# A written list of visits, relu evictions over two banks, and x loads as words of the list

## The chip, the core and the metric

The kernel runs on one core of one Trainium2 chip. The metric is the device time of one launch in microseconds. Before the change three runs took 314.47, 314.52 and 314.9 us (median 314.52).

## The reference

Two stages, of which the second takes the first's output as its tokens:

```python
# x: (4, 12544, 128), inducing: (32, 128), w1, w2: (128, 1024), w_out: (1024, 128)
def mab(q, kv):
    s = scale * (q @ kv.transpose(0, 2, 1))
    s = s - s.max(-1, keepdims=True)
    a = np.exp(s)
    a /= a.sum(-1, keepdims=True) + 1e-09
    return a @ kv
h = mab(I, x)                     # 32 inducing points look at all of x, per batch
attn = mab(x, h)                  # each token looks at the 32 rows of h
g = np.maximum(attn @ w1, attn @ w2)
out = g @ w_out
```

With max(a, b) = a + relu(b - a) the second stage is attn @ (w1 @ w_out) + relu(attn @ (w2 - w1)) @ w_out. Since attn is e2 / sum(e2) times h, with e2 the exponentials of 32 scores per token, the kernel multiplies h into the weights first: hwd = h @ (w2 - w1), 32 x 1024 per batch, and m1 = h @ (w1 @ w_out), 32 x 128. The division by sum(e2) is left to the end.

## The kernel before

A batch has 98 chunks of 128 tokens. Tokens are worked on in 28 blocks of up to 16 chunks. In a block each of the four row tiles of TensorE (32 of its 128 rows, called a quarter q) has its own 4 chunks, or fewer in the blocks at the ends of batches: the 32 scores per token of quarter q lie on partitions 32q to 32q + 31 of the tile `e2`.

The work of one block, by the letters of the list:

- `s` (`stage`, L698 on): scores of the block on TensorE in four column tiles, then one exponential on ACT into `e2`.
- `p` (`phase`): a visit to the row tiles. Up to four units, one per quarter, each a product of 32 rows of `hwd` with `e2`, 512 columns, into a PSUM bank of its own. Matmuls of different quarters run side by side, those of one quarter one after the other. Each unit's bank is then evicted with a relu into `relus` in SBUF: on ACT (L1110) or, where the bit of the word's second number is set, on DVE (L1107). 784 units in all. With fewer than four units, a visit also takes along the linear part `m1` of one open group, 4 short matmuls on that group's row tile (L1205 records both).
- a number n: n products of the final matmul (`final_one`, L989), relu chunk (128 x 128) times a 128 x 128 piece of w_out, over all 128 rows. The products of one quarter of one block are a group: 8 per chunk, 3136 in all, 108 groups, each in a PSUM bank. When the group's linear part is in as well, `evict_group` multiplies by the reciprocal sums into one of 6 buffers (`osbs`) on DVE (L1024) or ACT (L1031), and SP stores it.
- `g` (`turn_e2`): SP turns `e2` by a DMA transpose, GpSimd adds up the 32 exponentials per token and takes the reciprocal (L776, L780). Blocks without it have their sums from TensorE and DVE instead (`dens`, L819, L829).
- `c`, `r`, `t`, `a`, `e`, `h`, `w`, `m`: the first stage of the next batch, its scores (L399) and exponentials (L413), their transposes, the sum over x (L458), then h, hwd and m1. `x` turns a piece of x into `xT`, a DMA transpose on SP. `H`, `V`, `W` are batch 0's last part of hwd, the turn of w1 and its product with w_out.

TensorE thus changes between three ways of working: over all rows, in row tiles, in column tiles. The order of TensorE's work, and with it that of all engines, is the string `ORDER`. Which units a visit takes and which PSUM banks everything uses is not in the string: `Clock` keeps expected times of the engines and banks while the program is generated, `pick` takes the units needed first, and each takes the bank that is expected to come free first. Where the clock expects a wait, `keep_busy`, `dummies` and `fill` put empty matmuls (L945, L619).

The loads of x come from GpSimd as DMAs that cast to 16 bits, 7 per batch, into a ring of 12 buffers; buffer (7b + i) % 12 holds part i of batch b. Batch 1's are issued in the head of the program. Those of batch b + 1 for b = 1 and 2 stand at the end of `pool_accum` (word `a1.5`, `a2.5`), all seven together, behind a small copy of the sum just made (`pace`), so that GpSimd does not run ahead of them.

The eviction of one unit, with the bank in `src` and the home of the block's quarter in `dst`:

```python
dst = blk.relu[q][:, 0 : NJB * w4 * 128].rearrange("p (j t) -> p j t", j=NJB)
dst = dst[:, u * jpb : (u + n) * jpb, 128 * t0 : 128 * (t0 + w)]
src = psall[:, bi, :].rearrange("p (j t) -> p j t", j=jpb)
nc.scalar.activation(out=dst, in_=src, func=AF.Relu)
```

`phase` has a third number that would hold a unit back and evict it with the same quarter's next one; no word of `ORDER` uses it.

Of the kernel before, what the change touches and what calls it, by code (L numbers as in the profile page):

```python
# [9 lines left out]
F16 = mybir.dt.float16  # L10
# [6 lines left out]
INF = 1e9  # L17
# [90 lines left out]
class Quarter:  # L108


    def __init__(self, b, c0, w):
        self.b, self.c0, self.w = b, c0, w
        self.subs = {1: [1], 2: [2], 3: [2, 1], 4: [4]}[w]


class Block:


    def __init__(self, quarters, full=()):
        self.quarters = quarters  # L120
        self.width = max(qu.w for qu in quarters if qu)
        self.b = [qu.b for qu in quarters if qu][0]
        self.staged = None
        self.first = None
        self.divided = 0.0
        self.rp = None
        self.units = []
        self.done = {}
        self.relu = {}
        self.last_group = {}  # L130
        self.groups = []
        for q, qu in enumerate(quarters):
            jobs = []
            t0 = 0
            for w in qu.subs if qu else []:
                for u in range(2 * w):
                    jobs.append((q, t0, w, u))
                t0 += w
            self.units.append(jobs)
            if qu:  # L140
                self.groups.append(Group(self, [(q, t) for t in range(qu.w)], q in full))


class Group:
    def __init__(self, blk, chunks, full):
        self.blk, self.chunks, self.full = blk, chunks, full
        self.q = chunks[0][0]
        self.bank = self.ps = None
        self.started = self.linear = False
        self.order, self.parts = [], []  # L150
        for q, t0, w, u in blk.units[self.q]:
            jpb = 4 // w
            self.parts.append((t0, u))
            self.order += [(jpb * u + jj, t0 + t) for jj in range(jpb) for t in range(w)]
# [3 lines left out]
def kernel(  # L158
# [37 lines left out]
    relus = [big.tile([128, 2, 4096], F16, name=f"relus{q}", tag=f"relus{q}") for q in range(4)]  # L196
    relu1 = [big.tile([128, 1024], F16, name=f"relu1_{q}", tag=f"relu1_{q}") for q in range(2)]
    osbs = big.tile([128, NOUT, 4, C], F32, name="osbs", tag="osbs")

# [23 lines left out]
    def load_x(b, i, after=None):  # L223
        k0, n = parts[b][i]
        if after is not None:

            nc.gpsimd.tensor_copy(out=pace, in_=after)
        nc.gpsimd.dma_start(out=xn_at[b, i][:, 0:n, :], in_=xr[b, :, k0 : k0 + n, :])  # L228
        if b:
            issued = ck.on_pool(ck.pe, 0.55)  # L230
            if i == 0 and b > 1:
                ck.loading = issued - 0.55
            st[b]["ld", i] = ck.loading + 6.3 + 2.72 * i if b > 1 else 25.7 + 2.5 * i
# [4 lines left out]
    def transpose_x_dma(b, j):  # L238
# [3 lines left out]
        landed = ck.on_sp(st[b]["ld", i], "x7" if n == 7 else "x14")  # L242
        for k in range(k0, k0 + n):
            st[b]["T", k] = landed

    identity16 = consts.tile([128, 128], F16, name="identity16")
    head16 = relus[3][:, 0, :]
# [10 lines left out]
    wf = relus[0][:, 0, :].bitcast(F32)  # L258
    w1f, w2f = wf[:, 0:J], wf[:, J : 2 * J]
    w1s = relus[1][:, 0, :]  # L260
# [8 lines left out]
    pace = consts.tile([128, 1], F32, name="pace")  # L269

    with tc.manual_schedule(engines={ET.PE, ET.DVE, ET.Activation, ET.Pool, ET.SP}):

        xf = relus[2][:, 0, 0 : 256 * P1].bitcast(F32)
# [119 lines left out]
        def pool_scores(b, u):  # L393
            if u == 0:
                st[b]["es"] = smp.tile([128, NU], F32, name=f"es_{b}", tag="esu")
            bi, ps = bank([128, 512])
            ck.wait(ck.bank[bi], "p1")
# [10 lines left out]
            ck.feed(8)  # L408
            end = ck.run(0.226, "col")
# [3 lines left out]
            nc.scalar.activation(  # L413
                out=eu, in_=ps, func=AF.Exp, scale=scale, accum_out=st[b]["es"][:, u : u + 1]
            )
            ck.bank[bi] = ck.on_act(end, 0.575)
            st[b]["eu", u] = eu, ck.bank[bi]

        def pool_rest(b):

            bi, ps = bank([128, 512])
            ck.wait(ck.bank[bi], "p1")
# [8 lines left out]
            end = ck.run(0.029 * REST)  # L431
            et = etp.tile([128, P1, M], F16, name=f"et_{b}", tag="et")
            nc.scalar.activation(out=et[:, 0:REST, :], in_=ps[:, 0 : REST * M], func=AF.Exp, scale=scale)
            ck.bank[bi] = ck.on_act(end, 0.2)
            st[b]["et"] = et, ck.bank[bi]

        def pool_turn(b, u):
            eT = etp.tile([128, 8, 128], F16, name=f"eT_{b}_{u}", tag="eT", bufs=NEU)
            nc.sync.dma_start_transpose(eT, st[b]["pair", u // 2].rearrange("p v (j t) -> p (v j) t", j=4))
            st[b]["eT", u] = eT, ck.on_sp(st[b]["eu", u][1], "eT")  # L440

        def pool_accum(b, u):

            bi, ps = bank([128, 512])
            ck.wait(ck.bank[bi], "p1")
# [4 lines left out]
            if last:  # L450
                nc.vector.reduce_sum(out=acc[:, C : C + 1], in_=st[b]["es"], axis=AX.X)
                ck.on_dve(st[b]["eu", u][1], 0.1)
            eT = st[b]["eT", u][0]
            st[b]["sum", u] = True
# [12 lines left out]
            if last:  # L467
                et = st[b]["et"][0]
# [17 lines left out]
            ck.feed(64)  # L486
            end = ck.run(0.58 if last else 0.49, "col")
# [5 lines left out]
            ck.bank[bi] = ck.on_dve(end, 0.22)  # L493
            if last:
                st[b]["esrr"] = ck.bank[bi]
# [4 lines left out]
        def small_rep(b):  # L500

            bi, ps = bank([128, 512])
            ck.wait(ck.bank[bi], "p1")
            nc.tensor.matmul(out=ps[:, 0 : C + 1], lhsT=repd, rhs=st[b]["hacc"], start=True, stop=True)  # L504
            end = ck.run(0.28)
# [5 lines left out]
            ck.bank[bi] = st[b]["haccr"] = ck.on_dve(end, 0.45)  # L511

        def small_h(b):
            hT4 = smp.tile([C, 4, M], F16, name=f"hT4_{b}", tag="hT4")
# [808 lines left out]
```

## Time and profile before

| | |
|---|---|
| timed runs | 314.47, 314.52, 314.9 us |
| the profiled execution: span, first to last instruction | 312.9 us |
| granted TensorE clock, mean | 0.998 |
| TensorE busy | 306.0 us |
| DVE busy | 273.1 us |
| ACT busy | 280.7 us |
| GpSimd busy | 122.6 us |
| HBM read and written | 27.28 and 25.69 MB |
| issues of x loads in the head, first and last | 19.6 and 26.2 us (batch 1) |

The profile's own execution has no separate time; its span stands for it, and the timed runs lie 1.6 us above the span. In a row of a group, the numbers behind the bar are the busy time in us, the mean duration of one instruction in ns, and the idle time of the engine just before such instructions with what ended it. In a row of the timeline stand the start, the time until the last of the row's instructions ends, the engine, and how many instructions of that kind followed each other. TensorE's durations overlap: the distance from one row's start to the next is what a piece of work takes.

### The profile page before, as it was taken

The numbers are of one execution on the slowest core, as the hardware profiler recorded it, in microseconds if no ns is written. First come the engines' busy times: TensorE is split into PE (matmuls) and PEld (weight loads), VectorE is DVE, ScalarE is ACT, GpSimd is POOL, SyncE is SP. The second block draws the span as 40 slices with busy tenths as digits, with TensorE's granted clock in tenths as the row PEclk, the third lists the DMA queues.
The fourth block names the chain that finished last, engine by engine and source line by source line (L and its number), as shares of the span: only waits on it lengthen the run. The fifth ranks groups of instructions, "written<-read, shape, count | busy, mean of one in ns | idle before, by whom it ended". The sixth has DMA issues, their size and how long they took to land.

```text
span 312.9 us, 12567 instructions
## 1 busy us (share of the span) xinstructions
PE 306.0 (98%) x5316; PEld 239.4 (77%) x5316; DVE 273.1 (87%) x485; ACT 280.7 (90%) x581; POOL 122.6 (39%) x183
## 2 busy tenths in 40 slices
PE   6999999999999999999999999999999999999996
PEld 2875777777877777778877887778778877788885
DVE  2458999999889999988999998999999899989894
ACT  3668999999989989999999999989999899998875
POOL 7374007910530006677500565139205743288000
PEclk9999999999999999999999999999999999999999
DMA  7999999999399999989699999993422522342223
GB/s 206 208 255 203 218 214 192 167 231 232 107 204 244 256 212 202 212 199 218 136 241 256 185 241 200 194 229 114 131 86 103 153 102 87 118 130 103 103 88 136
DMA packets 80793, 55.69 MB, mean 178 GB/s; under 512 B 62272, under 2 KB 65632, under 8 KB 80736
## 3 DMA queue, kind: packets, MB, share of 16 engines
q1 hardware_dynamic: 74768, 41.19, 56.5%
q0 software_dynamic: 5968, 13.70, 22.6%
q8 instruction: 41, 0.67, 0.9%
q14 instruction: 16, 0.13, 0.1%
HBM read 27.28 MB, written 25.69 MB: 169 GB/s over the span
## 4 chain that ended last, share of the span: by engine, by line
PE 94%; DMA 3%; DVE 1%; issue 1%; POOL 0%; ACT 0%; POOLq 0%
PE psall L989 61%; PE psall L1205 23%; DMA xn<-in_x_dram 3%; PE psall L712 2%; PE psall L458 1%; PE psall L399 1%; PE psall L309 1%; PE psall L371 1%; PE psall L325 1%; DVE relus L1107 1%; PE psall L571 1%; PE psall L504 0%; PE psall L362 0%; DVE hwd L575 0%; PE psall L819 0%
## 5 line engine op out<-in xcount | busy, mean ns | idle before, releaser
L1110 ACT ACTIVATE relus<-psall 128x512 f16<-128x512 f32 x468 | 239.2, 620 | 15.4 <-PE psall L1205 14.4
L1107 DVE TENSOR_SCALAR relus<-psall 128x512 f16<-128x512 f32 x308 | 195.5, 683 | 16.6 <-PE psall L1205 15.7
L989 PE MATMUL psall<-woutp,relus 128*128 128x128 f16 x3104 | 203.7, 220 | 0.0
L989 PEld LDWEIGHTS <-relus 128*128 128x128 f16 x3104 | 174.9, 98 | 33.1 <-issue 27.3
L1205 PE MATMUL psall<-e,hwd 32*128 32x512 f16 (+2 forms) x840 | 81.1, 362 | 0.0
L776 POOL TENSOR_TENSOR half<-ed 128x256 f32<-128x256 f16 (+2 forms) x22 | 13.4, 611 | 145.5 <-DMA ed<-e 145.5
L780 POOL TENSOR_TENSOR rd<-den,minus 128x16 f32<-128x16 f32 (+2 forms) x22 | 57.8, 2628 | 1.7
L1024 DVE TENSOR_TENSOR osbs<-psall,rd 128x512 f32<-128x512 f32 (+1 forms) x80 | 50.9, 637 | 4.3 <-PE psall L1205 1.3
L1205 PEld LDWEIGHTS <-hwd 32*128 32x128 f16 x880 | 27.9, 91 | 11.7 <-issue 2.3
L1205 PE MATMUL psall<-m,e 32*128 32x128 f16 x372 | 36.6, 216 | 0.0
L1205 PEld LDWEIGHTS <-e 32*128 32x128 f16 x372 | 22.2, 92 | 9.6 <-issue 2.0
L776 POOL TENSOR_TENSOR half<-half 128x32 f32<-128x32 f32 (+4 forms) x66 | 21.4, 324 | 5.2
L228 POOL DMA_DIRECT2D xn<-in_x_dram x32 | 17.8, 569 | 5.7 <-DMA xn<-in_x_dram 4.3
L1024 DVE TENSOR_TENSOR osbs<-psall,rp 128x512 f32<-128x512 f32 (+3 forms) x24 | 15.6, 649 | 0.5 <-PE psall L1205 0.4
L313 DVE COPY xT<-psall 128x512 f16<-128x512 f16 (+3 forms) x12 | 5.7, 485 | 8.6 <-PE psall L309 8.4
L413 ACT ACTIVATE eu<-psall 128x512 f16<-128x512 f32 x18 | 10.8, 612 | 0.3 <-PE psall L399 0.2
L725 ACT ACTIVATE e<-psall 128x512 f16<-128x512 f32 (+2 forms) x21 | 10.9, 574 | 0.1
L316 ACT COPY xT<-psall 128x768 f16<-128x768 f16 (+3 forms) x10 | 5.8, 576 | 4.6 <-PE psall L309 4.5
L309 PE MATMUL psall<-identity,xn 128*128 128x128 f16 x98 | 7.5, 219 | 1.5 <-DMA xn<-in_x_dram 1.0
L712 PE MATMUL psall<-xT,hT 128*32 128x512 f16 (+3 forms) x110 | 8.4, 362 | 0.0
L309 PEld LDWEIGHTS <-xn 128*128 128x128 f16 x98 | 5.5, 97 | 3.1 <-DMA xn<-in_x_dram 1.4
L399 PE MATMUL psall<-xT,inducingT 128*32 128x512 f16 x72 | 6.4, 381 | 0.0
(114 smaller groups left out, 129.8 us busy)
## 6 DMA issues: line engine op xcount, KB each, us to landing
out_dram<-osbs SPq DMA_DIRECT2D x90, 256.0 KB, 2.9
xn<-in_x_dram POOLq DMA_DIRECT2D x24, 448.0 KB, 9.9
out_dram<-osbs SPq DMA_DIRECT2D x10, 128.0 KB, 4.3
relus<-in_moe_w_dram POOLq DMA_DIRECT2D x4, 256.0 KB, 5.7
xn<-in_x_dram POOLq DMA_DIRECT2D x4, 224.0 KB, 10.3
xT<-xn SPq DMA_TRANSPOSE x33, 4.3
relus<-in_x_dram SPq DMA_DIRECT2D x1, 512.0 KB, 4.0
relus<-in_x_dram SPq DMA_DIRECT2D x1, 384.0 KB, 4.4
```

What stands on the lines that cost most here:

```text
L228: nc.gpsimd.dma_start(out=xn_at[b, i][:, 0:n, :], in_=xr[b, :, k0 : k0 + n, :])
L309: nc.tensor.transpose(ps[:, j, :], xn[:, g + j, :], identity16)
L413: nc.scalar.activation(out=eu, in_=ps, func=AF.Exp, scale=scale, accum_out=st[b]["es"][:, u : u + 1])
L712: nc.tensor.matmul(out=ps[32 * q : 32 * (q + 1), 128 * t : 128 * (t + n)], lhsT=hq, rhs=xT[:, c : c + n, :], start=True, stop=True, tile_p ...
L725: nc.scalar.activation(out=blk.e2[:, 0 : 128 * wd], in_=ps[:, 0 : 128 * wd], func=AF.Exp, scale=st[0]["rs"] if blk.b == 0 else scale,)
L776: nc.gpsimd.tensor_tensor(out=dst, in0=cur[:, :, 0:n], in1=cur[:, :, n : 2 * n], op=ALU.add)
L780: nc.gpsimd.tensor_tensor(out=rp[:, 0:wd, :].rearrange("p t q -> p (t q)"), in0=den[:, 0 : 4 * wd], in1=minus1[:, 0 : 4 * wd], op=ALU.pow,)
L989: nc.tensor.matmul(out=g.ps[lo:hi, 128 * c : 128 * (c + 1)], lhsT=relu[:, lo:hi], rhs=woutp[:, jb, :], start=not g.started, stop=(state["m ...
L1024: nc.vector.tensor_mul(osb[:, 0:m, :], g.ps[:, 0 : m * C].rearrange("p (s c) -> p s c", s=m), g.blk.rp[:, t0 : t0 + m, q : q + 1].broadcas ...
L1107: nc.vector.tensor_scalar(out=dst, in0=src, scalar1=0.0, scalar2=None, op0=ALU.max)
L1110: nc.scalar.activation(out=dst, in_=src, func=AF.Relu)
L1205: nc.tensor.matmul(**seq.pop(0))
```

## The change

The clock's part in the order is gone: `ORDER` becomes `PLAN`, in which every visit names its units, their banks and the engine of each eviction, and every other word its bank. The words:

- `p` and then three characters a unit: quarter, bank, and `a` (ACT), `v` (DVE) or `+`. A `+` joins the unit to the next one: both are evicted by one instruction, of the next unit's engine. `l` adds the linear part of the group now being worked on, `L` that of the first finished group that still lacks it. Digits behind a colon give the order in which the matmuls are issued.
- `o` opens a group in a bank, `d` is a number of products, `n` a denominator by TensorE, `l` with two numbers a load of x.

The homes of the relus become one tile of 64 slots of 512 columns, 16 slots a quarter, so that a pair of units of two quarters can be written by one instruction with a stride between the two slots. 125 pairs take the place of 250 of the 784 single evictions: 87 on ACT and 38 on DVE. Evictions of groups on ACT become 8 instead of 4.

Loads of batches 2 and 3 are words between the others, and `pace` is gone. GpSimd's queue has them in the order of the list among the `g` words' sums. `l2.0`, `l2.1` and `l2.2` stand before the first `g`. 24 `g` words do something, 22 before, and 16 small matmuls make denominators, 24 before. Empty matmuls are left only where `H` and `W` name them: two and none. `Quarter`, `next_job`, `pick`, `flush`, `phase`, `keep_busy`, `final_one` and the rest of the clock's bookkeeping in the list's part are removed. The head of the program up to the list does the same as before.

```diff
-    relus = [big.tile([128, 2, 4096], F16, name=f"relus{q}", tag=f"relus{q}") for q in range(4)]
+    slots = big.tile([128, 64, 512], F16, name="relus", tag="relus")
...
-            if last and b + 1 < B:
-                for i in range(7):
-                    load_x(b + 1, i, acc[:, C : C + 1] if i == 0 else None)
...
+        def relu_home(blk, q):
+
+            if blk.relu[q] is None:
+                w = blk.widths[q]
+                small = w == 1 and 0 < blk.index < len(blocks) - 1
+                if small:
+                    blk.relu[q] = (relu1[q % 2], None)
+                else:
+                    base = 16 * q + 8 * (homes[q] % 2)
+                    homes[q] += 1
+                    blk.relu[q] = (slots[:, base : base + 2 * w, :].rearrange("p j t -> p (j t)"), base)
+            return blk.relu[q]
...
+        def relu_out(parts, vector):
+            if len(parts) == 2:
+                (a, ba), (z, bz) = [(home[1] + unit[2], bi) for home, unit, bi, _, _ in parts]
+                assert a < z and ba < bz
+                dst = slots[:, a : z + 1 : z - a, :]
+                src = psall[:, ba : bz + 1 : bz - ba, :]
+            else:
+                (home, _), (t0, w, u), bi, w4, _ = parts[0]
+                jpb = 4 // w
+                dst = home[:, 0 : NJB * 128 * w4].rearrange("p (j t) -> p j t", t=128 * w4)
+                dst = dst[:, u * jpb : (u + 1) * jpb, 128 * t0 : 128 * (t0 + w)]
+                src = psall[:, bi, :].rearrange("p (j t) -> p j t", j=jpb)
             if vector:
                 nc.vector.tensor_scalar(out=dst, in0=src, scalar1=0.0, scalar2=None, op0=ALU.max)
-                t = ck.on_dve(ready, (0.604, 1.141)[n - 1])
             else:
                 nc.scalar.activation(out=dst, in_=src, func=AF.Relu)
-                t = ck.on_act(ready, (0.484, 0.915)[n - 1])
...
+        def visit(word):
+
+            word, _, turns = word.partition(":")
+            lines = word[len(word.rstrip("lL")) :]
+            picks = [word[k : k + 3] for k in range(0, len(word) - len(lines), 3)]
...
+            busy, turns = [0] * 4, [int(c) for c in turns]
+            while any(seq for _, _, seq in rows):
+                k = min((k for k in range(len(rows)) if rows[k][2]), key=lambda k: busy[rows[k][0]])
+                k = turns.pop(0) if turns else k
+                q, cols, seq = rows[k]
                 nc.tensor.matmul(**seq.pop(0))
+                busy[q] += cols
...
+            k = 0
+            while k < len(made):
+                n = 2 if made[k][4] == "+" else 1
+                relu_out(made[k : k + n], made[k + n - 1][4] == "v")
+                k += n
...
+        PLAN = """
+        s6 p15v s0 x1.0 p11v p27a32a H4.2.0 V3.6 p05v20a p01v17a W2.0 p14a26a33v p20a m0.5 o7 d4 n2 d4
+        p01v24a33v p25v36a p32aL o0 d16 o1 d6 x1.1 p04v33aLl l2.0 x1.2 p06v27a35a:102 d17 p00v12+23a34a d1 o7
+        d16 p16a25v p00vl p02+13a21a:102 d16 l2.1 o4 d6 p16v25al p02+13a20v:120 x1.3 d10 n7+ d4 p01v x1.4
+        p15a36v p10a p17v p02a23a l2.2 d12 o5 d7 p01v20a36al d12 x1.5 p02v17a23a34v p30v s6 d11 p01a17a22a33v d2
+        o4 d15 g3 p00+11v26a33a s7 d16 p05a12v36vl p00+11a33a d1 o7 d26 p02v15+26al p00+11a24v d6 o3 d20 c1.0.2
+        p04a25+36v p17a20v31al:1023000 x1.6 d12 o2 d13 s4 x1.7 p05+26a37al p01v30v d19 c1.1.3 p04+15v20+31a
...
+        d17 o1 d13 p02+13a27v35a p06v20a34vl:10230100 d19 o7 d11 p12a23v36a p15a24v30al:0012312 d5 o1 d20
+        p02+13a36al p04v25v37a d12 o0 d16 o5 d5 p03+24aLl p02a11v26+37v:1032132 d19 p00a11a23v34a d8 o2 d16 o3
+        d1 p06v17v30aL p01v15a24al:1203023 d15 o2 d17 p00a p16a25v37a p14v21a33a d15 o6 d24 o0 d16 o5 d8
+        """
```

More of the change, by code (lines that the diff above doesn't have):

```diff
@@ L412, in pool_scores, with pool_rest @@
             eu = st[b]["pair", u // 2][:, u % 2, :]
[L413 to L422, printed above, removed]
+            nc.scalar.activation(out=eu, in_=ps, func=AF.Exp, scale=scale, accum_out=st[b]["es"][:, u : u + 1])
+        def pool_rest(b, bi):
+            ps = main_bank(bi)
             for j in range(REST):
@@ L596, in small_m1 @@
-        def small_m1(b):
-            bi, ps = bank([128, 512])
-            ck.wait(max(ck.bank[bi], st[b]["hT4r"]), "p1")
+            sl = slice(512 * step, 512 * (step + 1))
+            ps = main_bank(bi)
+            nc.tensor.matmul(out=ps, lhsT=st[b]["hT4"], rhs=w21[:, sl], start=True, stop=True)
+            if not scalar:
+                nc.vector.tensor_copy(out=st[b]["hwd"][:, sl], in_=ps)
+            else:
+                nc.scalar.copy(out=st[b]["hwd"][:, sl], in_=ps)
+        def small_m1(b, bi):
+            ps = main_bank(bi)
@@ L605, in small_m1 @@
+            for o, r in outs:
                 if b == 0:
```

850 lines of the change are left out of this document (297 added, 553 removed).

## The prediction

> **What bounds the kernel now.** I read the page first, then the waits, then stretches of time, then the timeline around single visits.
>
> ```profile
> span 312.9 us, 12567 instructions
> PE 306.0 (98%) x5316; PEld 239.4 (77%) x5316; DVE 273.1 (87%) x485; ACT 280.7 (90%) x581; POOL 122.6 (39%) x183
> PE 94%; DMA 3%; DVE 1%; issue 1%; POOL 0%; ACT 0%; POOLq 0%
> L1110 ACT ACTIVATE relus<-psall 128x512 f16<-128x512 f32 x468 | 239.2, 620 | 15.4 <-PE psall L1205 14.4
> L1107 DVE TENSOR_SCALAR relus<-psall 128x512 f16<-128x512 f32 x308 | 195.5, 683 | 16.6 <-PE psall L1205 15.7
> ```
> The second line is busy time by engine, the third the shares of the chain that ended last, the last two the relu evictions. TensorE carries the chain. ACT and DVE are close behind it, and what little they idle they idle for TensorE's row matmuls, not the other way round.
>
> ```profile
> 22.70:30.00 7.30, 6.80 (x91) 3.83 (x90) 5.69 (x12) 6.35 (x15) 4.02 (x7) 1.00 1.06 197
> 30.00:60.00 30.00, 30.00 (x483) 21.96 (x478) 29.57 (x52) 29.33 (x61) 10.97 (x15) 1.00 1.07 198
> 210.00:240.00 30.00, 30.00 (x545) 23.85 (x542) 27.75 (x53) 28.13 (x59) 15.17 (x21) 1.00 0.36 113
> ```
> Columns: stretch, length, then busy time of PE, PEld, DVE, ACT, POOL, the granted clock, the DMA share, GB/s. From 30 us on PE is busy for 30.00 of 30.00 at full clock. So the time is a sum of TensorE work, and the list wins only by needing less of it; it loses wherever TensorE has to wait. The view of waits has no row of PE waiting for a relu eviction of 0.5 us or more in total, so the old list pays next to nothing there.
>
> What a piece of TensorE work costs is read off the timeline (start, length, engine, instructions):
>
> ```profile
> 150.56 0.40 PE L1205 MATMUL psall<-e,hwd 32*128 32x512 f16 x4
> 150.89 0.95 PE L989 MATMUL psall<-woutp,relus 128*128 128x128 f16 x14
> ...
> 152.43 1.50 PE L989 MATMUL psall<-woutp,relus 128*128 128x128 f16 x24
> ...
> 153.86 0.60 PE L1205 MATMUL psall<-e,hwd 32*128 32x512 f16 x5
> ...
> 154.29 1.29 DVE L1107 TENSOR_SCALAR relus<-psall 128x512 f16<-128x512 f32 x2 [0.32 <-PE psall L1205]
> 154.41 0.84 PE L989 MATMUL psall<-woutp,relus 128*128 128x128 f16 x12
> ```
> A product (L989) takes (1.50 - 0.95)/10 = 0.055 us. A visit of one round (each row tile used once) takes 150.89 - 150.56 = 0.33 us, one of two rounds 154.41 - 153.86 = 0.55, so a round is 0.22 and leaving the row tiles 0.11. 24 products and the way into the next visit take 153.86 - 152.43 = 1.43, of which 24 x 0.055 = 1.32 are products: 0.11 to enter, and I use 0.10. A visit thus costs **0.21 us plus 0.22 per round**.
>
> **The change part by part, TensorE's demand.** Products stay (3136 in both lists). Row work stays (784 relu units and the linear parts), but is bundled otherwise. Old list: 164 visits; taking for each the fullest of its four row tiles, 241.5 rounds. New list, counted the same way: 148 visits (102 of two rounds, 44 of one, 2 of three), 254 rounds. Perfectly even tiles would need 220 in either. So:
> - 16 visits fewer: 16 x 0.21 = -3.4
> - 12.5 rounds more: 12.5 x 0.22 = +2.75
> - changes between full and column tiles that no visit lies between: 19 before, 23 after, at about 0.10: +0.4
>
> The headline (fewer visits) is given back by fuller tiles; it nets -0.25. Two small things come on top.
>
> ```profile
> 25.26 0.81 PE L619 MATMUL psall<-warm 128*128 128x512 f16 x3
> 26.09 0.41 DVE L646 COPY relus<-psall 128x512 f16<-128x512 f16 x1
> 26.55 0.45 PEld L662 LDWEIGHTS <-relus 128*128 128x128 f16 x8 [0.98 <-DVE relus L646]
> ...
> 27.65 0.25 PE L819 MATMUL psall<-ones_q,e_first 128*128 128x4 f16 x4
> 27.77 0.38 PE L989 MATMUL psall<-woutp,relus 128*128 128x128 f16 x4
> 27.98 0.22 PE L945 MATMUL psall<-warm 128*128 128x128 f16 x1
> 28.22 0.56 PEld L989 LDWEIGHTS <-relus 128*128 128x128 f16 x10 [0.19 <-ACT relus L1110]
> ```
> Between V and W (the turn of w1 and its product with w_out) the old list runs three empty matmuls and then waits; the new one has two short visits there, so 3 x 0.22 = 0.66 us of nothing becomes work, while the rest of the wait stays. The empty matmul at 27.98 (0.24 to the next) is gone. Denominators on TensorE: 24 small matmuls become 16, at (27.77 - 27.65)/4 = 0.03 each, -0.25; for that two more blocks go to GpSimd, which lies idle for over half the time. Sum: -0.25 - 0.66 - 0.24 - 0.25 = **-1.4 us**, with 0.5 either way for visits whose matmuls don't interleave as my rounds assume.
>
> **The two-bank evictions.** 125 pairs (87 on ACT, 38 on DVE) replace 250 of the 784 single ones. No row of before has 1024 columns.
>
> ```profile
> 149.41 4.51 ACT L1110 ACTIVATE relus<-psall 128x512 f16<-128x512 f32 x9
> ...
> 140.09 1.29 DVE L1107 TENSOR_SCALAR relus<-psall 128x512 f16<-128x512 f32 x2
> L316 ACT COPY xT<-psall 128x768 f16<-128x768 f16 x4 | 3.2, 799 | 2.6 <-PE psall L309 2.6
> L316 ACT COPY xT<-psall 128x384 f16<-128x384 f16 x4 | 1.9, 480 | 1.8 <-PE psall L309 1.7
> L1031 ACT ACTIVATE osbs<-psall,rd 128x128 f32<-128x128 f32 x10 | 3.1, 383 | 2.0 <-issue 1.0 <-PE psall L963 0.9
> L1024 DVE TENSOR_TENSOR osbs<-psall,rd 128x256 f32<-128x256 f32 x8 | 3.3, 417 | 1.6 <-ACT osbs L1031 1.1 <-ACT relus L1110 0.6
> ```
> ACT: 384 columns more cost 0.319 us (the two copies), 0.425 for 512, so a pair takes 0.620 + 0.425 = 1.05; from L1031 to L1110 the slope is smaller (0.237 for 384) and gives 0.94; two singles back to back, which is the upper end, take (4.51 - 0.62)/8 + 0.62 = 1.11. DVE: 256 columns more cost 0.683 - 0.417 = 0.266, so 1.21; two singles take 1.29. I take 1.05 and 1.21, as the copies run to the greatest width. That frees about 0.06 per ACT pair and 0.08 per DVE pair, 8 us over both engines. Since neither is the bound, I cost the gain at nothing: TensorE's own work hides it.
>
> [...]
>
> The price is that a pair holds **two banks for longer**. An eviction starts 0.21 us after its round (153.86 + 0.22 to 154.29, DVE row above), and TensorE goes on 0.05 after it (26.50 to 26.55). A bank is free 0.21 + 0.62 + 0.05 = 0.88 after its round with a single ACT eviction, 1.31 with a pair. Between two visits with n products lie 0.21 + 0.055 n us. So a bank can be written again in the very next visit without a wait after 12 products, with a pair only after 20. Old list: 474 units go into a bank that the visit just before used, and 13 evictions stand less than 12 products before such a use, 0.8 us short in all. New list: 578 units; 19 single ones are 2.2 us short in all and 20 pairs 3.5 us, together 5.7. What is queued behind such a wait is the whole of TensorE. Bounds: 0 (a bank of the first of two rounds is done 0.22 earlier, and one late bank delays all that come after it, so that they find theirs free), and 5.7 - 0.8 = 4.9 if each shortage is paid. I take about half, **+2.5**.
>
> **The loads as words.** l2.0 to l2.2 write buffers 2 to 4 of xn, last read by batch 0's head, so GpSimd does not wait at them: they go out behind batch 1's last load, near 27 us. In the old kernel batch 2's seven went out together after a1.5, behind the small copy into `pace`. SP's queue holds the stores and the turns of x.
>
> ```profile
> L228 POOL DMA_DIRECT2D xn<-in_x_dram x7: 538/556/571, 19.6 to 26.2; - x7
> DMA to landing us min/median/max: 6.8/9.5/15.0
> ...
> out_dram<-osbs SPq DMA_DIRECT2D x6, 256.0 KB, 7.8
> ...
> out_dram<-osbs SPq DMA_DIRECT2D x22, 256.0 KB, 2.0
> ```
> Rows one and two: batch 1's loads, last landing at 26.2 + 15.0 = 41.2, one per (41.2 - 26.4)/6 = 2.5 us. Third: stores of a block part while batch 2's loads run (85 to 107 us) land after 7.8 us; last: with none running (240 to 303), after 2.0. Three more loads stretch the slow time to 41.2 + 3 x 2.5 = 49 us. 108 groups leave in some 285 us, one per 2.6, so the ring of six output buffers covers 5 x 2.6 = 13 us, more than 7.8. I cost it at 0; with the cover gone, see the third case.
>
> **Sum.** -1.4 + 2.5 = +1.1. The profiled span is 312.9; the timed runs (314.47, 314.52, 314.9) lie 1.6 above it, which I leave. 314.5 + 1.1 = **315.6 us**.
>
> **The rivals.**
> 1. The waits stay away and the smaller demand is all that counts: 314.5 - 1.4 = 313.1. For it: ACT and DVE are relieved, and the old list's 0.8 us of shortage shows up in no row. Against: 5.7 is seven times that. It decides below 1.4 us of waits. This is the other side of my forecast.
> 2. The early loads hold up output. Six turns of x now stand ahead of or between the first stores on SP; store 1 lands after x1.0. If a store takes 7.8 us and the turns ahead of it come on top, the seventh group's multiplication on DVE waits for its buffer, the relus behind it wait too, and x1.2 comes late for c1.0. That group is due after 176 products, at 285/3136 us each from 27.8 on near 44 us; the slow time ends at 49, so the price lies between 0 and 5, and I take 3, as the first store need not be the last thing to land: 315.6 + 3 = 318.6. [...]
> 3. The pair does not do what it says: its output spans slots of two row tiles with a stride, and if products of the slots between wait for it too, each pair costs TensorE a good part of its 1.05 us: 125 x 0.5 = 60, 375 us. Nothing in before shows such a store.
>
> **How the numbers follow.** Forecast (slower by some waits) 0.50, first rival 0.32, second 0.15, third 0.03. The forecast's own range is 314.6 (waits 1.5) to 317.5 (waits 4.4). A measurement here can tell 0.2%, 0.6 us, from no change: same is 313.9 to 315.15. The forecast's low edge gives same 0.08, the rest slower; the first rival gives faster 0.28, same 0.04. Slower 0.60, same 0.12, faster 0.28. Eight in ten: 312.8 (first rival with 0.3 to spare) to 318.8 (second).
>
> **What would show it.** Right: PE idle or stretched inside visits, waits of row matmuls for ACT and DVE relus of 1 to 4 us in all, most behind pairs; 148 stretches of L1205's successor; pair rows near 1050 and 1210 ns. Wrong: visits at 0.33 and 0.55 throughout (first rival); DVE waiting for a store near 46 us, or TensorE for xT at c1.0 (second); products waiting for an ACT pair that wrote other slots (third). A pair at two singles' price, or a granted clock under 1.00, would break the sum itself.

## The result, and the profile after

The new kernel takes 330.2 us (330.18 and 330.20) against 314.61 for the old one on the same chip; the ratio is 1.049 [1.047, 1.051], and the loss 15.6 us. Two further runs of the new kernel, at 336.6 and 337.9, are over 1.5% above the fastest and are not in the ratio, and the ranges below leave out such runs of the variants too. The predicted sign was right, the size was not: 315.6 us was forecast, and 330.2 lies far outside 312.8 to 318.8.

The page of the new kernel, in the order of the lines shown of before (span, busy time by engine, shares of the chain that ended last, relu evictions on ACT and DVE). PE is TensorE, PEld its weight loads, DVE VectorE, ACT ScalarE, POOL GpSimd. In the new kernel L945 is the row matmuls, L827 the products, L381 the scores of the first stage, L860 and L867 the evictions of groups on DVE and ACT, L874 the stores, L216 the loads and L224 the turns of x, L411 and L681 the turns of the exponentials of the first and second stage, L694 the reciprocals on GpSimd; in the variants the numbers are shifted a little:

```profile
span 328.4 us, 12501 instructions
PE 312.0 (95%) x5304; PEld 242.1 (74%) x5304; DVE 272.7 (83%) x448; ACT 276.8 (84%) x499; POOL 131.3 (40%) x193
PE 77%; DMA 14%; DVE 4%; issue 2%; POOL 1%; SPq 1%; ACT 0%; DVEq 0%; POOLq 0%
L891 ACT ACTIVATE relus<-psall 128x512 f16<-128x512 f32 (+1 forms) x374 | 232.7, 708 | 25.7 <-PE psall L945 24.3
L889 DVE TENSOR_SCALAR relus<-psall 128x512 f16<-128x512 f32 (+1 forms) x277 | 197.5, 757 | 22.3 <-PE psall L945 18.6
```

ACT is busy for 3.9 us less than before, DVE for 0.4 less; that is not where the time went. The chain shows more: DMA's share of it rises from 3% to 14%, DVE's from 1% to 4%. The view by stretches of time says where (columns as in the prediction: PE, PEld, DVE, ACT, POOL, granted clock, DMA share, GB/s):

```profile
30.00:60.00 30.00, 27.86 (x417) 19.94 (x418) 23.92 (x38) 25.14 (x46) 1.62 (x4) 0.94 1.10 215
60.00:90.00 30.00, 24.36 (x359) 17.96 (x361) 20.47 (x32) 20.18 (x39) 8.81 (x11) 0.89 1.16 179
90.00:120.00 30.00, 28.41 (x547) 22.59 (x535) 25.08 (x45) 25.20 (x46) 10.44 (x17) 1.00 0.89 169
120.00:150.00 30.00, 30.00 (x485) 22.79 (x483) 27.84 (x42) 28.89 (x53) 14.95 (x19) 1.00 1.11 225
```

PE is idle for 2.1, 5.6 and 1.6 us in the three stretches between 30 and 120, and in two of them the granted clock is under 1. From 120 on it is busy for 30.00 of 30.00 again. So nearly all of the loss lies between 30 and 120 us. The waits of those stretches (us in total, times, longest):

```profile
PE psall L381 <- DMA xT<-xn: 5.6, 1, 5.6
...
DVE osbs L860 <- DMA out_dram<-osbs: 2.4, 1, 2.4
DVE osbs L860 <- POOL rd L694: 2.3, 1, 2.3
PE psall L945 <- DVE osbs L860: 2.1, 1, 2.1
...
PE psall L827 <- DVE osbs L860: 1.3, 1, 1.3
```

Each happens once. None of them is for a relu eviction, and what TensorE waits for behind each of them is a DMA: a turn of x, a store, the turn of `e2` that the sums on GpSimd stand behind.

**The first stall**, by the timeline (start, length, engine, instructions; in brackets the idle time before and its releaser; SPq is SP's queue of DMA issues, and its length is how long SP stood at them):

```profile
26.25 1.65 SPq L224 DMA_TRANSPOSE xT<-xn  x1
29.16 0.53 POOL L216 DMA_DIRECT2D xn<-in_x_dram  x1 [1.16 <-PE psall L945]
...
30.79 1.27 SPq L224 DMA_TRANSPOSE xT<-xn  x1
32.10 12.36 SPq L874 DMA_DIRECT2D out_dram<-osbs  x1
48.85 0.69 DVE L860 TENSOR_TENSOR osbs<-psall,rp 128x512 f32<-128x512 f32 x1 [2.36 <-DMA out_dram<-osbs]
49.59 0.37 PE L945 MATMUL psall<-e,hwd 32*128 32x512 f16 x1 [2.09 <-DVE osbs L860]
49.89 2.49 PE L827 MATMUL psall<-woutp,relus 128*128 128x128 f16 x26
52.31 0.62 PE L381 MATMUL psall<-xT,inducingT 128*32 128x512 f16 x4
```

The landings are in the views of the lines themselves: first the turns x1.0 (22.2 us) and x1.1 (18.6), then the four loads from 26.4 to 29.2, the last of batch 1 and l2.0 to l2.2.

```profile
L224 SPq DMA_TRANSPOSE xT<-xn x2: 1267/1460/1654, 26.3 to 30.8; - x2
DMA to landing us min/median/max: 18.6/20.4/22.2
```

```profile
L216 POOL DMA_DIRECT2D xn<-in_x_dram x4: 533/562/576, 26.4 to 29.2; - x4
DMA to landing us min/median/max: 14.8/17.6/19.3
```

x1.0 lands at 26.3 + 22.2 = 48.5, in the moment that l2.2 does (29.2 + 19.3). Two stores stand behind it, and the second one's issue alone holds SP for 12.4 us. At 46.5 DVE has no output buffer left and waits 2.4 us; TensorE, which needs a bank that DVE should have emptied, waits 2.1. Then TensorE takes 2.42 us (49.89 to 52.31) for 26 products and the way into the next piece, where 26 x 0.055 + 0.1 = 1.5 was the price before. The windows give the reason, a granted clock (third number from the end) of 0.61 and 0.54:

```profile
50.00:52.00 2.00, 2.00 (x25) 2.00 (x25) 1.33 (x3) 0.00 (x0) 0.00 (x0) 0.61 1.65 265
52.00:54.00 2.00, 2.00 (x21) 0.89 (x20) 0.40 (x1) 0.99 (x3) 0.00 (x0) 0.54 0.68 143
```

What the DMA engines do in that time, counted from the trace's DMA records (packets of all 16 engines in each 2 us):

```
from us   of loads, 3584 bytes   of turns, 256 bytes
38               105                   124
40               109                   119
42               105                   122
46                21                   446
48                 0                  1288
```

While the loads were in flight, load and turn packets started in nearly equal numbers, 105 to 109 and 119 to 124 in 2 us. A load packet took 0.285 us of its engine (the median), a turn's 0.03, and the turns got some 60 packets a us. A turn of seven chunks is 896 packets (x1.0 to x1.2 have 2688 of 256 bytes in the trace, from 30.2 to 50.0 us), 15 us at that pace by estimate, and the first one started 3.9 us behind the issue of x1.0. With the loads out of the way such packets ran ten times as fast, 1288 in the 2 us from 48 on.

**The second stall** is the same with l2.3, issued at 63.3 and landed 12.0 us later; x1.8, issued a quarter of a us before it, takes 13.0, and SP stands 6.8 us at the turn behind it:

```profile
63.08 3.06 SPq L224 DMA_TRANSPOSE xT<-xn  x1
63.33 0.62 POOL L216 DMA_DIRECT2D xn<-in_x_dram  x1
...
66.24 6.81 SPq L411 DMA_TRANSPOSE eT<-eu  x1
...
76.10 0.61 PE L381 MATMUL psall<-xT,inducingT 128*32 128x512 f16 x2 [5.64 <-DMA xT<-xn]
76.64 2.53 PE L827 MATMUL psall<-woutp,relus 128*128 128x128 f16 x22
```

TensorE stands for 5.6 us in front of the scores of c1.3 and then needs 2.53 us for 22 products, where 24 took 1.50 before. **The third**, near 108 us, is the wait for L694's reciprocals: the turn of g6's `e2` (98.3 to 105.3) runs beside l2.4 and l3.0 (95.0 to 104.1), GpSimd's sums come late, and DVE and TensorE wait 2.3 and 1.3 us. The clock stays at 1.00 there (the row from 90 to 120).

### The profile page after: what moved, and what is told of

Read it like the earlier page. It is cut to its first block, busy times and chain, and to the rows that moved or that the text cites. A ratio compares the mean times of both kernels' runs of the same rounds, so it can differ in the third digit from the quotient of the medians.

```text
span 328.4 us, 12501 instructions
## 1 busy us (share of the span) xinstructions
PE 312.0 (95%) x5304; PEld 242.1 (74%) x5304; DVE 272.7 (83%) x448; ACT 276.8 (84%) x499; POOL 131.3 (40%) x193
## 4 chain that ended last, share of the span: by engine, by line
PE 77%; DMA 14%; DVE 4%; issue 2%; POOL 1%; SPq 1%; ACT 0%; DVEq 0%; POOLq 0%
PE psall L827 49%; PE psall L945 19%; DMA out_dram<-osbs 6%; DMA xT<-xn 4%; DMA xn<-in_x_dram 3%; DMA ed<-e 2%; DVE relus L889 2%; PE psall L637 2%; PE psall L381 2%; PE psall L426 1%; PE psall L288 1%; DVE osbs L860 1%; PE psall L350 1%; SPq L224 1%; PE psall L304 1%
## 5 line engine op out<-in xcount | busy, mean ns | idle before, releaser
L891 ACT ACTIVATE relus<-psall 128x512 f16<-128x512 f32 (+1 forms) x374 | 232.7, 708 | 25.7 <-PE psall L945 24.3
L889 DVE TENSOR_SCALAR relus<-psall 128x512 f16<-128x512 f32 (+1 forms) x277 | 197.5, 757 | 22.3 <-PE psall L945 18.6
L827 PEld LDWEIGHTS <-relus 128*128 128x128 f16 x3104 | 177.3, 99 | 37.8 <-issue 34.4
L827 PE MATMUL psall<-woutp,relus 128*128 128x128 f16 x3104 | 203.0, 221 | 1.4 <-DVE osbs L860 1.3
L945 PE MATMUL psall<-e,hwd 32*128 32x512 f16 (+2 forms) x840 | 82.8, 364 | 2.5 <-DVE osbs L860 2.1
L690 POOL TENSOR_TENSOR half<-ed 128x256 f32<-128x256 f16 (+2 forms) x24 | 14.7, 611 | 152.4 <-DMA ed<-e 152.4
L860 DVE TENSOR_TENSOR osbs<-psall,rd 128x512 f32<-128x512 f32 (+2 forms) x86 | 55.3, 644 | 12.8 <-PE psall L827 6.4
L694 POOL TENSOR_TENSOR rd<-den,minus 128x16 f32<-128x16 f32 (+2 forms) x24 | 63.7, 2654 | 1.9
L945 PEld LDWEIGHTS <-hwd 32*128 32x128 f16 x880 | 28.6, 91 | 15.1 <-issue 3.5
L945 PE MATMUL psall<-m,e 32*128 32x128 f16 x372 | 36.8, 218 | 0.0
L945 PEld LDWEIGHTS <-e 32*128 32x128 f16 x372 | 21.5, 93 | 5.9 <-issue 0.7
L690 POOL TENSOR_TENSOR half<-half 128x32 f32<-128x32 f32 (+4 forms) x72 | 23.3, 324 | 5.6
L216 POOL DMA_DIRECT2D xn<-in_x_dram x32 | 18.1, 572 | 6.2 <-DMA xn<-in_x_dram 4.2
L381 PE MATMUL psall<-xT,inducingT 128*32 128x512 f16 x72 | 7.4, 401 | 5.6 <-DMA xT<-xn 5.6
L860 DVE TENSOR_TENSOR osbs<-psall,rp 128x512 f32<-128x512 f32 (+2 forms) x14 | 9.2, 655 | 2.9 <-DMA out_dram<-osbs 2.4
```

What stands on the lines that cost most here:

```text
L381: nc.tensor.matmul(out=ps[32 * g : 32 * (g + 1), :], lhsT=inducingT, rhs=xT_tiles[b % 2][:, U * u + 4 * g : U * u + 4 * (g + 1), :], start ...
L690: nc.gpsimd.tensor_tensor(out=dst, in0=cur[:, :, 0:n], in1=cur[:, :, n : 2 * n], op=ALU.add)
L694: nc.gpsimd.tensor_tensor(out=rp[:, 0:wd, :].rearrange("p t q -> p (t q)"), in0=den[:, 0 : 4 * wd], in1=minus1[:, 0 : 4 * wd], op=ALU.pow,)
L827: nc.tensor.matmul(out=g.ps[:, 128 * t : 128 * (t + 1)], lhsT=home[:, 128 * (jb * w4 + t) : 128 * (jb * w4 + t + 1)], rhs=woutp[:, jb, :], ...
L860: nc.vector.tensor_mul(osb[:, 0:n, :], g.ps[:, 0 : n * C].rearrange("p (s c) -> p s c", s=n), blk.rp[:, 0:n, q : q + 1].broadcast_to((128, ...
L889: nc.vector.tensor_scalar(out=dst, in0=src, scalar1=0.0, scalar2=None, op0=ALU.max)
```

## The experiments

Three theories were kept apart. Theory 1: DMA turns and stores starve beside loads in flight, and everything waits for them. Theory 2: the two-bank evictions keep TensorE from its banks. Theory 3: the list needs more of TensorE than the old one. Theories 2 and 3 are forms of what the prediction had put its money on.

### The loads moved back, in the new list

```diff
 late_first
-p04v33aLl l2.0 x1.2   d16 l2.1 o4   p02a23a l2.2 d12
+p04v33aLl x1.2        d16 o4        p02a23a d12
-p02+13a26v l2.4       x2.0 p02a g6  s3 s0 s4 x2.1
+p02+13a26v l2.0 l2.1 l2.2 l2.4      p02a g6  s3 s0 s4 x2.0 x2.1
 late_second
-t1.1 d11 l2.3 p13a26vl              p02+13a26v l2.4
+t1.1 d11 p13a26vl                   p02+13a26v l2.3 l2.4
 late_both: the two together
```

> The new list with l2.0, l2.1 and l2.2 moved down to the place of l2.4 and x2.0 moved down to x2.1; l2.3 stays where the new list has it. Theory 1 (turns of x and stores starve while these loads run, SP stands at a store, then DVE and TensorE wait and the products after it run at half speed): the stall near 50 us goes, 5 us by the times at equal product counts (-0.7 at product 200 to +4.2 at 350), the stall near 76 us stays: 330.2 - 5 = 325, between 323 and 327. Theory 2 (the two-bank evictions make TensorE wait for banks) and theory 3 (the list itself needs more of TensorE): nothing moves, 330.2 within 1.

> The new list with only l2.3 moved down to the place of l2.4. Theory 1: the stall near 50 us stays, that near 76 us goes with the slow products behind it, +4.2 at product 350 to +12.1 at 450: 330.2 - 8 = 322, between 320 and 324. Theories 2 and 3: 330.2 within 1.

> The new list with l2.0 to l2.3 moved down to the place of l2.4 and x2.0 down to x2.1, everything else as it is. Theory 1: both stalls go; the five loads then run beside g6 and the stores near 85 to 100 us, where the new list already lost 2 us: 330.2 - 13 = 317, between 314 and 319. Theories 2 and 3: still 329 or more.

Measured: late_first 326.6 us (324.5 to 327.8), late_second 327.8 to 332.1, late_both 327.3 to 329.3. The first lies in theory 1's band, the other two don't, and late_second's runs lie around the 330.2 that theories 2 and 3 had said. The totals mislead, though, and even the hit is one by accident. What counts is the time at equal product counts, which is the same list in all of them. Here it is, taken from the starts of the product matmuls and set against the same list without any load of batches 2 and 3 (new_noload, below), with the later runs in the same table:

```
products          200   250   350   450   700   750  1000  1200  2000  3135
new_noload, us   46.2  50.6  61.2  70.3  94.9  98.8 121.4 140.7 212.3 309.8
new kernel       +0.5  +4.4  +4.4 +12.7 +12.7 +14.8 +14.8 +14.8 +14.8 +14.8
late_first       -0.2  -0.2  -0.2  +0.9  +0.9  +0.9  +9.8 +11.6 +11.6 +11.6
late_second      -0.1  +6.0  +6.0  +6.0  +6.0 +12.4 +12.4 +12.4 +12.4 +12.4
late_both        +0.1  +0.1  +0.1  +0.1  +0.1  +1.4 +10.6 +12.0 +12.0 +12.0
clear            -0.0  -0.0  -0.0  -0.0   0.0   0.0   0.0  +6.6 +20.7 +20.8
clear_two        +0.7  +0.7  +0.7  +0.7  +0.7  +0.7  +0.7  +2.6  +6.7  +7.2
```

The loss comes in steps, with nothing between them: 3.9, 8.3 and 2.1 us in the new kernel. Moving l2.0 to l2.2 takes the first step away, and all but 1.1 of the second with it, which I had not expected: x1.8 then took 8.4 us beside l2.3, not 13.0. Moving l2.3 alone takes the second away and leaves the first, which cost 6.1 us in that execution: TensorE waited 3.1 us and not 2.1, and lost 3.0 behind the wait and not 1.8; the mean granted clock of the run was 0.978, against 0.982. So the same stall cost 3.9 us in one execution and 6.1 in another, and these are prices of single profiled executions. With all moved, the list stands within 0.1 us of its own unloaded run through 700 products. But the moved loads meet other turns. In late_both x2.0 and x2.1 are issued behind six loads, three more follow while they are under way, and a store stands behind them; rows of the turns, the timeline and the waits of that kernel:

```profile
L224 SPq DMA_TRANSPOSE xT<-xn x2: 1312/1490/1667, 89.9 to 91.2; - x2
...
DMA to landing us min/median/max: 19.3/19.5/19.8
```

```profile
93.00 14.76 SPq L874 DMA_DIRECT2D out_dram<-osbs  x3
```

```profile
ACT osbs L867 <- DMA out_dram<-osbs: 8.2, 1, 8.2
...
PE psall L709 <- ACT osbs L867: 7.4, 1, 7.4
```

The same stall in another place, and a dearer one: turns of 19.5 us, a store issue that holds SP, an output buffer that comes late, this time for ACT, and 7.4 us of TensorE.

### The early loads alone, in the old kernel

```diff
 old_early: in the head, behind batch 1's loads; EARLY is 3
         for i in range(3, 7):
             load_x(1, i)
+        for i in range(EARLY):
+            k0, n = parts[2][i]
+            nc.gpsimd.dma_start(out=xn_at[2, i][:, 0:n, :], in_=xr[2, :, k0 : k0 + n, :])
 load_x, which keeps its bookkeeping
+        if b != 2 or i >= EARLY:
+            nc.gpsimd.dma_start(out=xn_at[b, i][:, 0:n, :], in_=xr[b, :, k0 : k0 + n, :])
```

> The old list with loads 0 to 2 of batch 2 issued right behind batch 1's loads near 27 us and left out of the seven at the end of a1.5; no pair, no other change of order. Theory 1: the first turns of x land when the last of these loads lands, near 48.5 instead of 42 us, stores wait beside them, and the kernel gets slower by 2 to 6 us: 318.5. Theories 2 and 3, by which the loads do no harm: 314.6 within 0.6.

320.7 us (320.1 to 321.1), 1.019 [1.017, 1.020] of the old kernel: no pair, no new list, and 6 us lost, 5.9 of them before product 350. That is theory 1's price, at its upper end. The timeline of that run:

```profile
53.90 0.59 PE L402 MATMUL psall<-xT,inducingT 128*32 128x512 f16 x1 [3.06 <-DMA xT<-xn]
...
54.42 2.10 PE L995 MATMUL psall<-woutp,relus 128*128 128x128 f16 x18
```

and its windows, with the granted clock again third from the end:

```profile
54.00:56.00 2.00, 2.00 (x17) 1.58 (x17) 0.19 (x1) 0.69 (x2) 1.44 (x3) 0.50 1.06 253
56.00:58.00 2.00, 2.00 (x20) 1.17 (x19) 1.40 (x3) 0.81 (x2) 1.81 (x3) 0.50 1.03 285
...
60.00:62.00 2.00, 2.00 (x38) 1.63 (x36) 2.00 (x5) 1.27 (x4) 1.61 (x6) 1.00 0.95 180
```

TensorE waits 3.1 us and is then at half clock for more than 5 us (0.50, 0.50 and 0.59 in the three windows from 54 to 60).

One load instead of three is the same edit with `EARLY` at 1:

> The old kernel with one load of batch 2 instead of three issued behind batch 1's. The last load lands 2.5 us later than in the old kernel, near 43.7, and the first turns of x with it; the scores of c1.0 come near 50 us. If lateness costs only past the cover (theory 1): 314.7 within 0.6. If every load beside the turns costs its share of the 5.5 us: 316.4.

315.9 us (314.5 to 316.8), 1.003 [1.001, 1.005]. The median lies above the 314.7 within 0.6 of theory 1 and below the 316.4 of the other reading, so the total does not decide. Through product 1000 the run stands within 0.2 us of the old kernel, as the cover theory has it; the profiled run then lost 1.5 us near 140, where a score waited 0.95 us for a turn of batch 2, and the fastest run (314.53) can't have lost that much, by its total. So c1.0 has cover for one more load and not for three; what delays the later turn in some of the runs was not followed up.

### The half clock

```diff
 old_early_busy: old_early, and in pool_scores
+            for _ in range(16 if (b, u) == (1, 0) else 0):
+                nc.tensor.matmul(out=ps, lhsT=warm[:, 0:128], rhs=warm, start=True, stop=True)
             for g in range(4):
```

> The run old_early with 16 empty matmuls of 512 columns, about 3.5 us, right in front of the four scores of c1.0, where TensorE stood idle for 3 to 4 us waiting for xT and then worked at a granted clock of 0.50 for some 5 us. Theory A (the clock falls because TensorE stood idle): the wait is filled, the clock stays near 1.00, and the 2.5 us lost to half speed come back: 320.1 - 2.5 = 317.6. Theory B (the clock falls for another reason, such as the DMA traffic): 320.1 to 321.

318.15 us (318.09 to 318.33), 2.5 us under old_early. Its timeline at the same place:

```profile
50.30 3.63 PE L402 MATMUL psall<-warm 128*128 128x512 f16 x16
53.86 0.40 PE L404 MATMUL psall<-xT,inducingT 128*32 128x512 f16 x4
54.19 1.18 PE L997 MATMUL psall<-woutp,relus 128*128 128x128 f16 x18
```

The scores still start at 53.9, since the turn is as late as before, but the 18 products behind them take 1.18 us and not 2.10, and the clock of every 2 us from 48 to 60 is 1.00, as in this row:

```profile
54.00:56.00 2.00, 2.00 (x34) 1.39 (x31) 0.97 (x2) 0.87 (x3) 1.55 (x4) 1.00 1.06 238
```

With TensorE kept busy the clock stayed at 1.00 beside 238 GB/s, where old_early had 0.50 beside 253: the idle time made the clock fall, not the traffic. The late turn thus cost 3.4 us with the clock kept up and 5.9 without (at product 350, against the old kernel). In the new kernel's first stall 2.1 us without a matmul were enough: its clock records have 0.50 from 50.4 to 53.9 us.

### The same lists without the loads

```diff
 old_noload, new_noload: in load_x
+        if b < 2:
             nc.gpsimd.dma_start(out=xn_at[b, i][:, 0:n, :], in_=xr[b, :, k0 : k0 + n, :])
 new_noload_single: that, and in visit
-                n = 2 if made[k][4] == "+" else 1
-                relu_out(made[k : k + n], made[k + n - 1][4] == "v")
+                n = 1
+                relu_out(made[k : k + 1], made[k + (made[k][4] == "+")][4] == "v")
```

> The old kernel without the fourteen loads of x for batches 2 and 3: these batches are computed from what batches 0 and 1 left in the buffers. It is the base for the next two runs. The old kernel keeps its loads out of the way, so it should hardly gain: 313.5 to 314.7.

> The new kernel without the same fourteen loads, everything else (list, pairs, order of the turns on SP) as it is. Theory 1 (the loads beside turns and stores cost all of it): the whole loss goes, within 1.5 us of old_noload; by the times at equal product counts (-0.7 at product 200, at par from 1000 on) about 0.5 below it, 313.5. Theory 2 (two-bank evictions block TensorE): 2.5 us or more above old_noload. Theory 3 (the list needs more of TensorE): above old_noload by what is left of 15 us.

> The run new_noload with each of the 125 pairs evicted as two single ones on the pair's engine. If the pairs' bank waits are the prediction's 2.5 us: 2.5 faster than new_noload. If the 8 us that pairs free on ACT and DVE matter: 1 to 4 slower. By clear against clear_single up to product 1000 (0.4 later at equal counts) I expect 0.3 to 1 slower.

old_noload 315.5 us (314.9 to 317.1), new_noload 315.1 (315.0 to 316.1), new_noload_single 316.0 (316.0 to 316.7); the old kernel on that chip 314.76. Both lie above what was expected, by 0.8 us (the upper end, 314.7) and 1.6 (313.5), yet it is their distance that counts. The old kernel gains nothing without its loads; by the medians it is 0.8 us slower, and why stays open. The new one loses nothing any more: 15 us come back with fourteen DMAs and no other change. That ends theories 2 and 3 as causes. Its chain by engine is that of the old kernel:

```profile
span 313.5 us, 12460 instructions
...
PE 94%; DMA 3%; issue 1%; DVE 1%; POOL 0%; ACT 0%; POOLq 0%; DVEq 0%
```

It also prices what the prediction had weighed. Splitting the pairs makes the kernel 0.9 us slower, so the pairs are a small gain. The time from one matmul's start to the next, summed from the first product on over everything but product after product (empty matmuls count with the products), is 114.8 us in old_noload, 114.8 in new_noload and 115.8 in new_noload_single.

### Loads laid out anew

```diff
 clear: late_both's moves, and besides
-t1.5 a1.3.5   p02+13a26v l2.4                   p00v16+27aL x2.2
+t1.5 g6 a1.3.5   p02+13a26v l2.0 l2.1 l2.2 l2.3 l2.4 l2.5 l2.6   p00v16+27aL x2.0 x2.1 x2.2
-x3.0 x2.10 l3.2  g11 t2.3 d1 l3.3  g13 l3.4 x3.1
+x2.10 l3.0  g11 x3.0 t2.3 d1 l3.1  g13 l3.2 x3.1
...
 clear_single: clear with the pairs split
 clear_two
+t1.5 l2.0 l2.1 l2.2 l2.3 l2.4 l2.5 l2.6 g6 a1.3.5   p00v16+27aL x2.0 x2.1 g8 x2.2
+t2.5 g13 l3.0 l3.1 l3.2 l3.3 l3.4
...
```

In clear l3.3 and l3.4 follow before x3.6; in clear_two x3.0 to x3.5 are spread over 84 products from the old place of x3.5 on.

> The new list with its pairs, visits and products as they are, but no DMA turn within reach of a burst of loads: l2.0 to l2.6 together at the place of l2.4, g6 in front of them, x2.0 and x2.1 down to x2.2, and l3.0 to l3.4 one at a time between x2.10 and x3.6. Theory 1: the stall that late_first and late_both still had near 105 us, behind x2.0 and x2.1 which took 19 us beside nine loads, goes as well; late_both stood 1.2 us behind the old kernel at product 750, before that stall, and the new list then ran at par with the old one to the end: 314.5 + 1 = 315.5, between 313.5 and 317.5. Theories 2 and 3 (two-bank evictions, the list's own demand): the loss of late_both stays, 326 to 329.

> The list of the run clear with each of the 125 pairs evicted as two single ones, on the engine of the pair, everything else alike. If pairs make TensorE wait for banks by as much as the prediction took (2.5 us): 2.5 us faster than clear. If the time they free on ACT and DVE counts (8 us over both engines, two engines close to full): slower than clear by 1 to 5 us. If neither: within 0.6.

> The new list with all loads and no turn within a burst that is wanted at once, laid out after the run clear and the times of new_noload: l2.0 to l2.6 behind t1.5 with the turn of g6 issued on SP ahead of their landing, x2.0, x2.1 and g8 at x2.2; l3.0 to l3.4 behind t2.5 and g13, and x3.0 to x3.5 spread over the 20 us after them. Theory 1 (only loads beside turns and stores cost): 315.1 as in new_noload plus what these turns still wait, 314.8 to 317.5, at par with the old kernel through product 1000 and again from 1600 on. If something of the list's own depended on the early loads: 320 or more.

clear 335.2 us (332.1 to 336.2), clear_single 332.3 to 333.6, clear_two 320.9 to 323.3, all misses in the total. The table shows what they are good for: through 1000 products clear is new_noload to 0.0 us, with seven loads in it, so the three stalls are fully accounted for by where loads and turns meet. Behind that my own new places did damage. In clear the turns of batch 2 came later than its scores wanted them, and SP stood at turns whose loads had not landed. The dearest step in clear, 8.6 us between 207 and 216 us, is a store once more: issued at 205.5 between two turns and with loads of batch 3 under way, it landed 7.7 us later, and DVE waited for its buffer:

```profile
DVE osbs L860 <- DMA out_dram<-osbs: 8.4, 1, 8.4
```

The run clear_two keeps half of the loss; these waits are left in it:

```profile
DVE osbs L860 <- POOL rd L694: 3.1, 2, 2.6
...
PEld L426 <- DMA eT<-eu: 2.2, 2, 1.5
PE psall L827 <- DVE osbs L860: 2.0, 1, 2.0
```

The pair question stays undecided between clear and clear_single, whose later stalls differ; new_noload_single decides it. No layout was found that carries the loads and beats the old kernel. new_noload says that there is little to find: even with no load at all the new list only equals the old one.

## Why the prediction was right or wrong

- **"I cost it at 0", of the loads as words: the step that failed.** It was worth 14.3 us, the three steps in the profiled execution. The loads' end was foretold well (49, measured 48.5), and the cover of the output buffers was compared with it, but with the wrong row beside it: 7.8 us is what a store took beside loads in the old kernel from 85 to 107 us, with no turn under way (its trace has no packet of 256 bytes from 81.6 to 107.6). The two stores behind x1.0 and x1.1 took 18.4 and 17.6, more than the 13 us that the six buffers cover. In the old kernel the turns of batch 2 were issued from 106.3 us on, when the last of its loads was landing (88.1 + 19.1 = 107.2). The nearest row was that of x1.0 and x1.1 in the old kernel:

```profile
L241 SPq DMA_TRANSPOSE xT<-xn x2: 1428/2238/3047, 32.9 to 38.0; - x2
...
DMA to landing us min/median/max: 7.5/8.3/9.1
```

  x1.0 landed at 32.9 + 9.1 = 42.0, 0.8 us behind batch 1's last load (41.2). Read as "turns land when loads end", that row and the prediction's own 49 give the late turn and the stores behind it.
- **The second rival had the mechanism and the first place,** DVE waiting for an output buffer near 46 us, and bounded it at 5; that stall cost 3.9 here and 6.1 in late_second. It stopped there. l2.3 and l2.4 with l3.0 stand beside turns too, for 8.3 and 2.1 us more, and no sentence of the prediction looked at them. Of the first price, 3.9, only 2.1 is waiting and nearly half is slow clock, which no term allowed for.
- **What loads did to a turn was not priced.** The prediction set a store beside loads (7.8 us) against one without (2.0), and had no such pair for a turn. While the loads ran, load and turn packets started in nearly equal numbers (105 and 124 in 2 us), and by these numbers that is what did the harm: a turn of seven chunks is 896 small packets, and about one load packet of 0.285 us (0.85 to 0.92 by the three counts) started for each of them.
- **Bank waits of +2.5 us: too large.** Two counts bound them, both by inference. The whole of new_noload lies between 0.4 below and 0.4 above old_noload (medians, profiled spans); with all of the summed -1.4, waits would be 1.0 to 1.8. From the first product on, everything but products took 114.8 us in both, where -0.25 for visits, rounds and changes and -0.25 for denominators were summed, which leaves 0.5. That the pairs are to blame for them is wrong: without pairs the same sum is 1.0 more. A pair held two banks for longer (1029 ns on ACT, where a single takes 610) but ended its second eviction sooner (two singles back to back took 1.11 us), and ACT and DVE, at 88% and 87% in new_noload, did matter a little. "I cost the gain at nothing" fell with it, by 0.9 us.
- **Demand of -1.4 us: counted right, its worth not settled.** The traces of old_noload and new_noload have 165 and 149 stretches of row matmuls, 16 fewer as summed. For the 0.9 at the start there is no clean reading: at product 200 new_noload is 1.1 us ahead of the old kernel, but with 47 row matmuls of 512 columns done against 50; at product 350, with 91 against 90, it is 0.3 ahead.
- **Durations of a pair: right.** 1029 and 1219 ns, for 1050 and 1210:

```profile
L891 ACT ACTIVATE relus<-psall 128x1024 f16<-128x1024 f32 x87 | 88.7, 1029 | 6.0 <-PE psall L945 5.2 <-ACT relus L891 0.6
L889 DVE TENSOR_SCALAR relus<-psall 128x1024 f16<-128x1024 f32 x38 | 46.2, 1219 | 5.1 <-PE psall L945 2.6 <-issue 2.3
```

  "No row of before has 1024 columns" was too broad: DVE has copies of 128x1024 out of 16-bit banks (L313, 692 ns). They are of one bank and would have misled: the pair on DVE took 1219.
- **First and third rival.** For the list alone, those 0.4 either way lie between the forecast's +1.1 and the first rival's -1.4. No product waited for a strided pair: the new kernel's view of waits, with rows down to 0.2 us, has none of L827 behind a relu eviction.

## What to carry to other kernels

Before a load is moved earlier, list every DMA that will be in flight beside it, the small-packet turns first, and give each the landing time of the last load instead of its own, as a first bound (x1.0 landed with l2.2, both at 48.5 us); then go down the queue that issues them and ask what stands behind. An off-path transfer that came late enough was paid for twice on TensorE, once as the wait and once as the slow clock after it: in old_early 5.9 us, of which 3.4 were left with the clock kept up. When a change loses time in steps, compare times at equal counts of a common instruction: totals of two repairs can agree with a theory by accident.

## What the runs showed of the hardware that was not expected

- Beside loads from GpSimd a DMA turn of seven chunks took 18.6 to 22.2 us in the first stall and 19.3 to 19.8 in late_both, and 7.5 to 9.1 in the old kernel, where the loads ended sooner; in new_noload, between 100 and 118 us and with no load in flight, 3.0 to 4.5:

```profile
L225 SPq DMA_TRANSPOSE xT<-xn x5: 1220/1289/1303, 103.4 to 113.6; - x5
...
DMA to landing us min/median/max: 3.0/3.0/4.5
```

- A turn of fourteen chunks, x1.8, took 13.0 us beside one load, 8.4 beside the same load in late_first, and 4.1 in late_both without it. The load itself landed after 12.0 us in the first case and 5.9 in the second, where it was issued 1 us ahead of the turn and not behind it. Why the two differ stays open.
- A store's issue held SP for 12.4 us while turns and loads were under way; in late_both three stores in a row held it for 14.8.
- The clock records show half clock behind idle times of TensorE of 2.00 us (clear, near 142), 2.09 (new kernel), 3.1 (old_early) and more, and none behind 1.32 (new kernel), 1.68 (clear) and 1.96 (clear_two); what decides between them stays open. In the new kernel it lasted for 3.4 us behind the 2.09 (50.4 to 53.9) and, beginning within an idle time of 5.64, for 6.8 (74.3 to 81.2); once it lasted for 10.2, behind 7.8 us in clear.
